# Value loads cut at 112 partitions instead of 115, and one more batch whose expert is chosen from its first token

## The chip, the core and the metric

The kernel runs on one core of a Trainium2 chip. The metric is the device time of one execution, in microseconds (us). The engines are TensorE (PE in the profile, its weight loads PEld), VectorE (DVE), ScalarE (ACT), GpSimd (POOL) and SyncE (SP). DMAs are issued by an engine's queue (SPq, ACTq); sixteen DMA engines move the data.

## What is computed

Eight batches. In each, 8 heads of packed attention (32 packed queries read 576 keys and values, then the 576 queries read the 32 packed results), and then a mixture of experts over the 576 tokens: every token is sent to an expert, which is two matrix products with a relu between.

```python
def sm_attn(qq, kk, vv):
    s = scale * np.matmul(qq, kk.transpose(0, 1, 3, 2))
    s = s - np.max(s, axis=-1, keepdims=True)
    a = np.exp(s)
    a = a / (np.sum(a, axis=-1, keepdims=True) + 1e-09)
    return np.matmul(a, vv)
p_packed = sm_attn(p, k, v)          # 8 batches, 8 heads, 576 tokens, 64 wide; 32 packs
out = sm_attn(q, p_packed, p_packed)
# x = out as [batch, token, 512]; E = 8 experts, w1 [512, 1024], w2 [1024, 512]
logits = np.einsum('bsd,de->bse', x, w_gate)
local_gate = 1.0 / (1.0 + np.exp(-np.einsum('bsd,de->bse', x, w_local).squeeze(-1)))
for s in range(S):
    fresh_e = int(np.argmax(logits[b, s]))
    e = fresh_e if s == 0 or local_gate[b, s] < 0.5 else prev_e
    prev_e = e
    h = np.maximum(x[b, s] @ w1[e], 0.0)
    out[b, s] = p[e] * (h @ w2[e])   # p: softmax of logits[b, s]
```

## The kernel before

The kernel counts on it that all tokens of a batch go to the expert of the batch's first token. It computes that one expert for all 576 tokens, and notes in `stray` whether any token would have gone elsewhere; only then does the branch `general` at the end (line 1053) run.

For each batch the work is a set of Python generators, which a planner (`weave`, line 994) interleaves into one fixed order per engine while the program is built:

- `loads` (line 324) issues the batch's inputs on SP's queue: values (`load_values`, line 277, two loads, for the even and the odd heads, into the tile `kv`), packed queries (`p_in`, line 315), keys and queries (`load_blocks`, line 289, four DMAs each at line 298, into the tile `qn`). Keys and queries come in runs of 32 floats.
- `turn_keys`, `scores` (L414), `keys` (transposes L461, product with the values L474, L489) and `queries` (L535, softmax on DVE and ACT at L565 to L582, then `a2h` and `a2l`, the high and low parts of the attention weights, at L588 and L591) do the attention of a batch.
- `gates` (line 684) computes the logits of all tokens (L692, L700). Out of them `choose` (line 618) takes the expert's number into a register of SP (`value_load`, L627).
- `early_choice` (line 629) takes the expert from the first token alone: it needs the packed results of both halves of the heads (`ppT`) and that token's queries (`q0`, products L642, a short softmax L650 to L665, product with the gate weights L672, argmax L681), and none of the batch's queries. Batches below `FIRST` use it: here 0 and 1. For them `gate_weights` (L607) makes the gate product; for the others L544 makes it inside `queries`.
- `weights` (line 783) waits for that register, then loads the expert's `w1` in two halves (`w1t`, L792) and `w2` in eight pieces (`w2raw`, L801). `pack_weights` multiplies `w1` with the packed results (L818) into `wph` and `wpl`, the weights of the first product.
- `chunks` (line 922) is the main stream: for every batch 8 chunks of 128 columns, each with the first product (`layer1`, L841), relu (L851, L856), the split of `w2` (`split`, L867, L869), and one chunk later the second product (`layer2`, L880, L885, L889). `store` (L920) writes the output.

TensorE executes in program order, so a matmul whose operands are late holds all that stand behind it. Ahead of batch 0's main stream the planner puts in matmuls that nobody reads (`keep_warm`, L211); how many is fixed when the program is built. SP's queue also runs in order: a DMA that waits, or the read of an expert's register at L627, holds the DMAs behind it.

What sets the order around the change, apart from data: a batch's loads start when the previous batch's are all issued and the expert of the one before that is known (line 339); each load needs a free buffer (4 `kv`, 3 `qn`, 2 `p_in`, 8 `w2raw`, 2 `w1t`); and line 348 holds the keys of batch `FIRST` until `w1` of the batch ahead of it has been issued.

576 tokens stand in the values' tile as 5 tokens per partition: 115 partitions hold 575, and partition 115 the last one. So each of the two loads of a batch is one DMA of 115 partitions (575 KB) and one of one partition (1 KB).

Of the kernel before, what the change touches and what calls it, by code (L numbers as in the profile page):

```python
# [19 lines left out]
B, H, S, D = 8, 8, 576, 64  # L20
# [4 lines left out]
TP = 96  # L25
NJ = S // TP
J3 = NJ // 2
NV, VP = 5, 116
HALF = S // 2

NT = HALF // 32
SPAD = 640
NB = SPAD // 128
FIRST = 2
NC = F // 128
TAIL = S - 512

# [118 lines left out]
def packed_attn_moe_kernel(  # L156
# [12 lines left out]
    nc = tc.nc  # L169
# [7 lines left out]
    def tile_(shape, dtype, name, tag=None):  # L177
        bufs = BUFS.get(tag or name, 2)
        x = sb.tile(shape, dtype, name=name, tag=tag or name, bufs=bufs)
        clock.follow(x.tensor.name, tag or name, bufs)  # L180
        return x
# [47 lines left out]
    nc.vector.memset(wgl, 0.0)  # L229
    q0 = [const.tile([64, H, 32], F32, name=f"q0_{x}") for x in range(FIRST)]  # L230
    for x in q0:
# [12 lines left out]
    def at(src, b):  # L244

        return src[b] if isinstance(b, int) else src[bass.ds(b, 1)].squeeze(0)
# [7 lines left out]
    def need(*tiles, slot=(), banks=0, when=None):  # L254
        slots = [(x, 1) if isinstance(x, str) else x for x in ((slot,) if isinstance(slot, str) else slot)]

        def ready():

            if (when is not None and not when()) or not all(clock.free_slot(*x) for x in slots):
                return None  # L260
            free = free_banks()
            if len(free) < banks:
                return None
            return max(clock.ready(tiles), free[banks - 1][0] if banks else 0.0, *(clock.slot(*x) for x in slots))
        ready.banks = banks
        return ready
# [10 lines left out]
    def load_values(src, b, Q):  # L277

        x = tile_([128, HQ, NJ * D], F32, "kv")
        clock.rate = 250.0  # L280
        rows = at(src, b).rearrange("(h q) s d -> q s h d", q=NQ)[Q]
        nc.sync.dma_start(
            out=x[:VP - 1, :, :NV * D].rearrange("p h (c d) -> p h c d", c=NV),
            in_=rows[:S - 1].rearrange("(p c) h d -> p h c d", c=NV),
        )
        nc.sync.dma_start(out=x[VP - 1:VP, :, :D], in_=rows[S - 1:S])
        return x

    def load_blocks(src, b):


        x = tile_([128, H, NT * 32], F32, "qn")
        rows = at(src, b).rearrange("h (c i r) (a j) -> r a i (h c) j", r=2, c=NT, a=2)
        clock.rate = 150.0
        for r in range(2):
            for a in range(2):
                ps_ = slice(64 * r + 32 * a, 64 * r + 32 * a + 32)
                nc.sync.dma_start(out=x[ps_].rearrange("i h (c j) -> i (h c) j", j=32), in_=rows[r, a])  # L298
        return x

    def load_packs(b, queues):

        x = tile_([TP, H, D], F32, "p_in")
        clock.rate = 150.0
        for z, queue in enumerate(queues):
            queue.dma_start(out=x[NP * z:NP * z + NP], in_=at(p, b).rearrange("h n d -> n h d"))
        return x

    def load_packs_by_half(b):

        x = tile_([128, H, D // 2], F32, "p_in")
        clock.rate = 130.0
        halves = at(p, b).rearrange("h n (a j) -> a n h j", a=2)
        for z in range(4):
            nc.sync.dma_start(out=x[NP * z:NP * z + NP], in_=halves[z % 2])
        return x

    def begin(b, st, early=False):
        st["b"], st["early"], st["first"] = b, early, isinstance(b, int) and b < FIRST
        st["gate"] = gate_all[b % 3 if isinstance(b, int) else 0]  # L320
        st["ppT"] = [None] * NQ
        st["quads"] = st["asked"] = st["scored"] = st["weighed"] = st["raised"] = 0

    def loads(st):

        b = st["b"]
        if st["early"]:
            st["p"] = load_packs(b, (nc.sync, nc.scalar, nc.scalar))

            clock.rate = 100.0  # L330
            with nc.allow_non_contiguous_dma(reason="512 elements"):
                for x in range(FIRST):
                    nc.scalar.dma_start(out=q0[x][:, :, 0:1], in_=q[x, :, 0:1, :].rearrange("h s d -> d h s"))
            nc.scalar.dma_start(out=wgl[:, :, 0:E], in_=w_gate.rearrange("(h d) e -> d h e", d=D))
            nc.scalar.dma_start(out=wgl[:, :, E:E + 1], in_=w_local.rearrange("(h d) e -> d h e", d=D))
            order = (("k", 0), ("k", 1), ("v", 0), ("v", 1), ("q", 0), ("q", 1))
        else:
            if isinstance(b, int):
                yield need(when=lambda: "loaded" in sts[b - 1] and (b < 2 or "ereg" in sts[b - 2]))
            order = (("v", 0), ("v", 1), ("p", 1), ("k", 1), ("q", 1))  # L340
        for name, Q in order:
            blocks = name in "qk" and not st["early"]
            if isinstance(b, int) and b == 1 and name == "p":

                yield need(when=lambda: len(sts[0].get("w1", ())) == 2)
            if isinstance(b, int) and b == 1 and name in FIRST_W2:
                yield need(when=lambda: len(sts[0].get("w2", ())) >= FIRST_W2[name])
            if isinstance(b, int) and b == FIRST and name == "k":

                yield need(when=lambda: len(sts[b - 1].get("w1", ())) == 2)  # L350
            yield need(slot="p_in" if name == "p" else "qn" if blocks else "kv")
            if name == "p":
                st["p"] = load_packs_by_half(b)
                continue
            x = {"k": k, "v": v, "q": q}[name]
            if blocks:
                st[name] = load_blocks(x, b)
            else:
                st[name, Q] = (load_tokens if st["early"] else load_values)(x, b, Q)
        st["loaded"] = True  # L360
# [633 lines left out]
    def weave(main):  # L994
# [3 lines left out]
        while main in threads or any(x.batch < 0 for x in threads):  # L998
            while loading < B and loading <= max(at_batch[0], 0) + AHEAD + 1:
                begin(loading, sts[loading], early=(loading == 0))  # L1000
                threads.append(Thread(loads(sts[loading]), loading, True))
                loading += 1
# [50 lines left out]
    with tc.If(found[0] > 0, label="general"):  # L1053
        rows_d = {}
        for name, src in (("codes", codes_all), ("fresh", fresh_all)):
            tp = bank()
            nc.tensor.transpose(
                out=tp[:B * NB, :128], in_=src.rearrange("a b n -> a (b n)"), identity=ident,
# [35 lines left out]
        with tc.For_i(0, B) as bi:  # L1094
            with tc.For_i(0, E) as ei:
                go = nc.values_load(todo[0:1, bass.ds(bi, 1), bass.ds(ei, 1)].rearrange("a b e -> a (b e)"), min_val=0, max_val=1)
                with tc.If(go > 0):
                    st = {}
                    begin(bi, st)
                    drain(slots(st), loads(st), turn_keys(st, 0), turn_keys(st, 1), scores(st, 0), scores(st, 1), keys(st, 0), keys(st, 1), turn_queries(st, 0), turn_queries(st, 1), queries(st, 0), queries(st, 1))  # L1100
                    drain(gates(st, expert=ei), weights(st), pack_weights(st))
                    col = sb.tile([128, NB], F32, name="col", bufs=1)
                    nc.sync.dma_start(out=col, in_=at(ec_d, bi).rearrange("(n t) -> t n", t=128))
                    want = sb.tile([128, 1], F32, name="want", bufs=1)
                    nc.vector.tensor_copy(out=want, in_=code[:, bass.ds(ei, 1)])
                    mask = sb.tile([128, NB], I32, name="mask", bufs=1)
                    nc.vector.tensor_scalar(out=mask, in0=col, scalar1=want, scalar2=None, op0=ALU.is_equal)
                    drain(chunks([(bi, st)], drain, mask))
# [28 lines left out]
```

## Time and profile before

| what | value |
|---|---|
| median of 3 runs | 446.18 us (444.81, 446.18, 743.2) |
| profiled execution | 443.56 us, of which span from first to last instruction 441.8 us |
| PE busy | 422.0 us, 96% of the span |
| DVE, ACT busy | 69%, 41% of the span |
| granted TensorE clock, mean | 0.984 |
| DMA queue of SP and others (q1) | 72.30 MB, 75.7% of sixteen engines |

Times in the rows count from the span's start. A timeline row gives start, duration, engine, line, operation and the count of merged instructions; in brackets stands the idle time of that engine just before, and what ended it. PE is busy nearly everywhere, so its time is to be read by stretches, together with the granted clock (1.00 is 2.4 GHz, 0.50 is 1.2 GHz).

### The profile page before, as it was taken

The numbers are of one execution on the slowest core, as the hardware profiler recorded it, in microseconds if no ns is written. First come the engines' busy times: TensorE is split into PE (matmuls) and PEld (weight loads), VectorE is DVE, ScalarE is ACT, GpSimd is POOL, SyncE is SP. The second block draws the span as 40 slices with busy tenths as digits, with TensorE's granted clock in tenths as the row PEclk, the third lists the DMA queues.
The fourth block names the chain that finished last, engine by engine and source line by source line (L and its number), as shares of the span: only waits on it lengthen the run. The fifth ranks groups of instructions, "written<-read, shape, count | busy, mean of one in ns | idle before, by whom it ended". The sixth has DMA issues, their size and how long they took to land.

```text
span 441.8 us, 9954 instructions
## 1 busy us (share of the span) xinstructions
PE 422.0 (96%) x3834; PEld 325.7 (74%) x3835; DVE 305.9 (69%) x838; ACT 179.4 (41%) x407; POOL 26.2 (6%) x56
## 2 busy tenths in 40 slices
PE   8959999999997999999999999999999999999995
PEld 7746877676785578767876888777876878778883
DVE  4584668968688659868975588868886588544332
ACT  1424243453341653355425354246335444344221
POOL 0001000110011001100110002000110002000000
PEclk9997999999999699999999999999999999999999
DMA  9888965996998779977997797659957030732003
GB/s 188 198 252 187 154 143 165 275 134 126 133 227 191 278 136 131 220 290 134 151 229 289 135 138 196 238 180 128 188 191 260 27 108 1 287 108 94 1 0 111
DMA packets 172448, 73.12 MB, mean 166 GB/s; under 512 B 142662, under 2 KB 151406, under 8 KB 172398
## 3 DMA queue, kind: packets, MB, share of 16 engines
q1 hardware_dynamic: 169742, 72.30, 75.7%
q8 instruction: 31, 0.51, 0.5%
q10 hardware_dynamic: 2656, 0.15, 0.5%
q14 instruction: 19, 0.16, 0.1%
HBM read 63.00 MB, written 9.44 MB: 164 GB/s over the span
## 4 chain that ended last, share of the span: by engine, by line
PE 80%; DMA 7%; DVE 6%; SPq 2%; issue 1%; ACT 1%; ACTq 0%; POOLq 0%; DVEq 0%; POOL 0%
PE acc L880 37%; PE bank L841 21%; PE bank L818 4%; DMA w1t<-in_moe_w_dram 4%; PE acc L885 3%; PE acc L889 3%; PE bank L414 2%; PE bank L474 2%; PE bank L461 2%; PE bank L535 2%; DMA qn<-in_k_dram 2%; SPq L298 2%; PE acc L211 1%; DVE qn L374 1%; DMA p_in<-in_p_dram 1%
## 5 line engine op out<-in xcount | busy, mean ns | idle before, releaser
L880 PE MATMUL acc<-w2s,h 128*128 128x512 f32 x768 | 210.8, 404 | 0.3 <-DVE h L856 0.3
L880 PEld LDWEIGHTS acc<-w2s,h 128*128 128x128 f32 x768 | 135.2, 189 | 35.6 <-issue 12.7
L851 ACT ACTIVATE h<-bank 128x288 fp32r<-128x288 f32 x128 | 52.8, 412 | 114.5 <-PE bank L841 104.2
L856 DVE SCALAR_TENSOR_TENSOR h<-bank,h 128x288 fp32r<-128x288 f32 (+2 forms) x192 | 61.5, 347 | 47.6 <-ACT h L851 47.2
L841 PEld LDWEIGHTS bank<-a2h,wph 128*128 128x128 f32 x256 | 46.3, 189 | 22.9 <-issue 4.0
L841 PE MATMUL bank<-a2h,wph 128*128 128x288 f32 x256 | 57.6, 306 | 1.9 <-DVE df L750 0.8
L841 PE MATMUL bank<-a2l,wph 128*128 128x288 f32 x256 | 55.2, 296 | 0.6 <-POOL a2l L591 0.6
L841 PE MATMUL bank<-a2h,wpl 128*128 128x288 f32 x256 | 55.0, 296 | 0.0
L869 DVE TENSOR_TENSOR w2s<-w2raw,w2s 128x512 fp32r<-128x512 f32 x64 | 47.1, 736 | 4.2 <-ACT w2s L867 4.1
L841 PEld LDWEIGHTS bank<-a2l,wph 128*128 128x128 f32 x256 | 41.2, 189 | 0.8 <-POOL a2l L591 0.8
L591 POOL TENSOR_TENSOR a2l<-a2t,a2h 128x576 fp32r<-128x576 f32 x15 | 21.8, 1454 | 331.4 <-ACT a2h L588 331.4
L841 PEld LDWEIGHTS bank<-a2h,wpl 128*128 128x128 f32 x256 | 41.2, 189 | 0.0
L867 ACT CAST w2s<-w2raw 128x512 fp32r<-128x512 f32 x64 | 39.5, 617 | 0.2
L825 ACT CAST wph<-bank 128x512 fp32r<-128x512 f32 x31 | 16.8, 589 | 37.2 <-PE bank L818 34.2
L828 DVE TENSOR_TENSOR wpl<-bank,wph 128x512 fp32r<-128x512 f32 x31 | 20.0, 684 | 16.1 <-ACT wph L825 16.1
L885 PE MATMUL acc<-w2s,h 128*128 128x512 f32 x64 | 26.8, 418 | 0.0
L889 PE MATMUL acc<-w2s,h 128*64 128x512 f32 x64 | 25.2, 394 | 0.0
L818 PE MATMUL bank<-w1t,ppT 64*32 64x512 f32 x248 | 20.0, 652 | 5.4 <-DMA w1t<-in_moe_w_dram 5.4
L211 PEld LDWEIGHTS acc<-warm 128*128 128x128 f32 x134 | 18.5, 220 | 3.7 <-issue 2.7
L211 PE MATMUL acc<-warm 128*128 128x128 f32 x134 | 20.1, 309 | 1.2 <-DVE warm L204 1.2
L553 DVE STREAM_TRANSPOSE sT<-bank 128x288 f32<-128x288 f32 x29 | 12.4, 463 | 12.1 <-ACT gate L551 9.7
L374 DVE STREAM_TRANSPOSE qn<-qn 128x1152 f32<-128x1152 f32 x14 | 18.9, 1350 | 2.5 <-DMA qn<-in_k_dram 2.5
(152 smaller groups left out, 414.0 us busy)
## 6 DMA issues: line engine op xcount, KB each, us to landing
w1t<-in_moe_w_dram SPq DMA_DIRECT2D x16, 1024.0 KB
w2raw<-in_moe_w_dram SPq DMA_DIRECT2D x64, 256.0 KB
out_dram<-o SPq DMA_DIRECT2D x32, 256.0 KB
qn<-in_k_dram SPq DMA_DIRECT2D x28, 288.0 KB
qn<-in_q_dram SPq DMA_DIRECT2D x28, 288.0 KB
kv<-in_v_dram SPq DMA_DIRECT2D x14, 575.0 KB
kv<-in_k_dram SPq DMA_DIRECT2D x2, 576.0 KB
kv<-in_v_dram SPq DMA_DIRECT2D x2, 576.0 KB
```

The costliest lines, as they stand in the source:

```text
L211: nc.tensor.matmul(out=warm_ps[:, :128], lhsT=warm, rhs=warm, start=True, stop=True)
L374: nc.vector.transpose(out=kT, in_=kT)
L591: eng.tensor_tensor(out=a2l, in0=a2t, in1=a2h.bitcast(F32), op=ALU.subtract)
L818: nc.tensor.matmul(out=ts[Q][32 * h:32 * h + 32, :], lhsT=st["ppT"][Q][rows, 32 * h:32 * h + 32], rhs=w1t[rows, h], start=True, stop=True,)
L841: nc.tensor.matmul(out=t[:, :HALF], lhsT=st["wp"][c // 4][wi][:, Q, fs], rhs=a2[ai][Q][:, ts], start=(n == 0), stop=(n == 5),)
L851: nc.scalar.activation(out=h[:, HALF * half:HALF * half + HALF], in_=t[:, :HALF], func=AF.Relu)
L856: nc.vector.scalar_tensor_tensor(out=h[:, dst:dst + z - a], in0=t[:, a:z], scalar=0.0, in1=h[:, HALF * half + a:HALF * half + z].bitcast(F32),
L867: nc.scalar.copy(out=w[:, 0], in_=raw)
L869: nc.vector.tensor_tensor(out=w[:, 1], in0=raw, in1=w[:, 0].bitcast(F32), op=ALU.subtract)
L880: nc.tensor.matmul(out=acc, lhsT=hs[hi], rhs=w[:, wi], start=(c == 0 and n == 0), stop=(c == NC - 1 and n == 2),)
L885: nc.tensor.matmul(out=acc, lhsT=h[:, 512:S + TAIL], rhs=w[:, 0], start=(c == 0), stop=False, skip_group_check=True,)
L889: nc.tensor.matmul(out=acc[0:TAIL], lhsT=h[:, 512:S], rhs=w[:, 1], start=False, stop=(c == NC - 1), skip_group_check=True,)
```

## The change

Three edits. The values' load of 115 partitions is cut into one of 112 and one of 3 partitions (`VW = 112`); the one of a single partition stays. `FIRST` goes from 2 to 3, so batch 2 too takes its expert from the first token, with a third `q0` tile that is cleared and loaded at the start. And the keys of batches 2 and 3 (before: of batch 2) wait in the planner's order until `w1` of the batch ahead is issued. Batch 0 loads its values by `load_tokens` and is not touched by the first edit.

```diff
-NV, VP = 5, 116
+NV, VP, VW = 5, 116, 112
 HALF = S // 2
...
-FIRST = 2
+FIRST = 3
...
         rows = at(src, b).rearrange("(h q) s d -> q s h d", q=NQ)[Q]
-        nc.sync.dma_start(
-            out=x[:VP - 1, :, :NV * D].rearrange("p h (c d) -> p h c d", c=NV),
-            in_=rows[:S - 1].rearrange("(p c) h d -> p h c d", c=NV),
-        )
+        for lo, hi in ((0, VW), (VW, VP - 1)):
+            nc.sync.dma_start(
+                out=x[lo:hi, :, :NV * D].rearrange("p h (c d) -> p h c d", c=NV),
+                in_=rows[NV * lo:NV * hi].rearrange("(p c) h d -> p h c d", c=NV),
+            )
         nc.sync.dma_start(out=x[VP - 1:VP, :, :D], in_=rows[S - 1:S])
...
-            if isinstance(b, int) and b == FIRST and name == "k":
+            if isinstance(b, int) and 2 <= b <= FIRST and name == "k":
                 yield need(when=lambda: len(sts[b - 1].get("w1", ())) == 2)
```

Every line behind the diff's third hunk is one number higher in the changed kernel. Up to batch 2's packed results TensorE's order is the same in both.

**SP's queue, from batch 3's values on, before** (`e` is batch 2's expert, taken from its gates; the `w1t` under it is batch 2's; `qn<-in_k` and `qn<-in_q` are batch 3's keys and queries):

```order
L282 DMA kv<-in_v_dram 115x4x320
L286 DMA kv<-in_v_dram 1x4x64
L315 DMA p_in<-in_p_dram 32x8x32 x4
L298 DMA qn<-in_k_dram 32x72x32 x4
...
L920 DMA out_dram<-o 64x512
L298 DMA qn<-in_q_dram 32x72x32 x4
L627 TENSOR_LOAD e_1822
L627 ISA x2
L792 ISA
L792 DMA w1t<-in_moe_w_dram 128x4x512
```

The same place in the change (`eix` is batch 2's expert from its first token):

```order
L283 DMA kv<-in_v_dram 112x4x320
L283 DMA kv<-in_v_dram 3x4x320
L287 DMA kv<-in_v_dram 1x4x64
L316 DMA p_in<-in_p_dram 32x8x32 x4
...
L921 DMA out_dram<-o 64x512
L628 TENSOR_LOAD eix
L628 ISA x2
L793 ISA
L793 DMA w1t<-in_moe_w_dram 128x4x512
...
L299 DMA qn<-in_k_dram 32x72x32 x4
L299 DMA qn<-in_q_dram 32x72x32 x4
```

Batch 3's keys and queries now stand behind the read of batch 2's expert, its `w1` and five pieces of its `w2`; before, they stood ahead of all of these.

**TensorE at the end of batch 1's main stream, before**: the scores of batch 3 (L414, two pairs) and batch 2's first product of weights (L818) in one block, with no chunk's matmul between:

```order
L889 MATMUL acc_1418<-w2s,h 64x512
L414 MATMUL bank_1924<-qn,p_in 32x288 x4
L414 MATMUL bank_1925<-qn,p_in 32x288 x4
L414 MATMUL bank_1942<-qn,p_in 32x288 x4
L414 MATMUL bank_1943<-qn,p_in 32x288 x4
L818 MATMUL bank_1966<-w1t,ppT 32x512 x4
L818 MATMUL bank_1967<-w1t,ppT 32x512 x4
L841 MATMUL bank_1988<-a2h,wph 128x288 x2
```

In the change the same scores of batch 3 (L415 there), by which time batch 2's main stream is under way:

```order
L842 MATMUL bank_2036<-a2h,wpl 128x288 x2
L881 MATMUL acc_2055<-w2s,h 128x512 x3
L415 MATMUL bank_2064<-qn,p_in 32x288 x4
L415 MATMUL bank_2065<-qn,p_in 32x288 x4
L881 MATMUL acc_2080<-w2s,h 128x512 x3
L881 MATMUL acc_2084<-w2s,h 128x512 x3
L415 MATMUL bank_2090<-qn,p_in 32x288 x4
L415 MATMUL bank_2091<-qn,p_in 32x288 x4
```

The two pairs of scores are apart, with products of the main stream between them. Batch 2's weights have gone forward into batch 1's main stream:

```order
L881 MATMUL acc_1370<-w2s,h 128x512 x3
L673 MATMUL bank_1674<-gate_103,et 32x32 x2
...
L881 MATMUL acc_1401<-w2s,h 128x512 x3
L819 MATMUL bank_1807<-w1t,ppT 32x512 x4
L819 MATMUL bank_1808<-w1t,ppT 32x512 x4
L886 MATMUL acc_1422<-w2s,h 128x512
```

L673 is the gate product of batch 2's first token and L819 the first use of its `w1`. Between these two stand 18 L842, 21 L881, one L886 and one L890; between L673 and batch 3's first L415 stand 60 L842, 60 L881, 16 L819, 16 of the gates' and 5 each of L886 and L890. For the batch before, both kernels have between L672 and L818 18 L841, 21 L880, 8 L535, one L885 and one L889, and from L672 to batch 2's first L414 54 L841, 60 L880, 16 L818, 8 L535, 16 of the gates' and 4 each of L885 and L889 (in the old line numbers).

## Rows read from the trace of the kernel before

**Rows 1.** The page: the granted clock of TensorE in 40 equal slices of the span, in tenths of full speed.

```profile
PEclk9997999999999699999999999999999999999999
```

**Rows 2.** Busy time by stretches; columns: stretch, its length, busy time of PE, PEld, DVE, ACT, POOL with the count of instructions, granted clock, mean share of the sixteen DMA engines, GB/s.

```profile
28.30:33.60 5.30, 0.01 (x1) 0.00 (x0) 5.15 (x13) 1.19 (x2) 0.00 (x0) 0.80 1.04 347
31.50:38.30 6.80, 4.61 (x28) 2.98 (x29) 3.26 (x8) 2.21 (x4) 0.33 (x1) 0.50 0.82 273
89.00:103.00 14.00, 12.32 (x89) 9.04 (x75) 10.71 (x37) 6.01 (x13) 1.62 (x5) 1.00 1.32 128
138.00:144.10 6.10, 3.74 (x47) 1.08 (x49) 5.78 (x21) 0.00 (x0) 0.00 (x0) 1.00 0.85 302
144.10:151.00 6.90, 6.75 (x28) 3.53 (x28) 5.15 (x14) 4.20 (x9) 0.00 (x0) 0.51 0.96 353
189.00:230.00 41.00, 40.83 (x390) 31.16 (x388) 32.02 (x77) 19.73 (x46) 3.74 (x6) 1.00 1.01 188
```

**Rows 3.** The same columns where loads of one kind fill the queue: batch 0's keys and values (96 partitions, 4:9), then batch 1's values (115 partitions, 21:23), `w1t` (128 partitions, 30:31), and batch 3's values (104:108).

```profile
4.00:9.00 5.00, 4.45 (x39) 4.26 (x38) 2.26 (x2) 1.28 (x1) 0.00 (x0) 1.00 1.14 243
21.00:23.00 2.00, 1.64 (x19) 1.41 (x18) 1.19 (x7) 2.00 (x6) 0.00 (x0) 1.00 0.33 120
30.00:31.00 1.00, 0.00 (x0) 0.00 (x0) 0.96 (x5) 0.00 (x0) 0.00 (x0) 1.00 1.03 373
104.00:108.00 4.00, 4.00 (x37) 3.04 (x36) 3.83 (x10) 1.33 (x4) 0.00 (x0) 1.00 0.33 121
```

**Rows 4.** SP's queue in order of time, while it issues batch 1's second value load and batch 0's `w1t`.

```profile
18.65 0.28 SPq L282 DMA_DIRECT2D kv<-in_v_dram  x1
18.98 3.11 SPq L286 DMA_DIRECT2D kv<-in_v_dram  x1
24.45 1.04 SPq L792 DMA_DIRECT2D w1t<-in_moe_w_dram  x2
```

**Rows 5.** TensorE in order of time, from batch 0's queries to its main stream.

```profile
24.92 3.39 PE L211 MATMUL acc<-warm 128*128 128x128 f32 x28
...
33.69 1.96 PE L818 MATMUL bank<-w1t,ppT 64*32 64x512 f32 x16 [5.38 <-DMA w1t<-in_moe_w_dram]
...
35.58 4.25 PE L211 MATMUL acc<-warm 128*128 128x128 f32 x24
...
41.14 0.43 PE L841 MATMUL bank<-a2l,wph 128*128 128x288 f32 x2
```

**Rows 6.** VectorE, ScalarE and GpSimd in order of time, on the way to the operands of that first L841.

```profile
33.00 0.84 DVE L582 STREAM_TRANSPOSE a2t<-sT 128x288 f32<-128x288 f32 x2
...
35.68 1.07 ACT L825 CAST wph<-bank 128x512 fp32r<-128x512 f32 x2 [6.18 <-PE bank L818]
...
36.63 1.26 ACT L588 CAST a2h<-a2t 128x576 fp32r<-128x576 f32 x2
...
37.35 0.76 DVE L591 TENSOR_TENSOR a2l<-a2t,a2h 128x576 fp32r<-128x576 f32 x1 [3.51 <-ACT a2h L588]
...
37.97 1.42 POOL L591 TENSOR_TENSOR a2l<-a2t,a2h 128x576 fp32r<-128x576 f32 x1 [36.25 <-ACT a2h L588]
...
38.02 1.28 DVE L828 TENSOR_TENSOR wpl<-bank,wph 128x512 fp32r<-128x512 f32 x2
```

**Rows 7.** From batch 1's early choice to batch 2's scores, TensorE, SP's queue and VectorE in order of time.

```profile
70.29 0.31 PE L672 MATMUL bank<-gate,et 128*32 128x32 f32 x4
...
72.61 1.07 SPq L792 DMA_DIRECT2D w1t<-in_moe_w_dram  x2
...
77.73 12.49 SPq L298 DMA_DIRECT2D qn<-in_k_dram  x4
...
79.30 1.09 PE L818 MATMUL bank<-w1t,ppT 64*32 64x512 f32 x16
...
96.28 1.38 DVE L374 STREAM_TRANSPOSE qn<-qn 128x1152 f32<-128x1152 f32 x1 [2.46 <-DMA qn<-in_k_dram]
...
99.91 0.69 PE L414 MATMUL bank<-qn,p_in 64*32 64x288 f32 x8
```

**Rows 8.** Batch 2's weights and batch 3's scores: SP's queue and TensorE in order of time.

```profile
137.63 1.01 SPq L792 DMA_DIRECT2D w1t<-in_moe_w_dram  x2
...
139.10 0.92 PE L414 MATMUL bank<-qn,p_in 64*32 64x288 f32 x16 [0.57 <-issue]
...
140.81 0.69 PE L414 MATMUL bank<-qn,p_in 64*32 64x288 f32 x8 [0.79 <-DVE gsm L759]
...
142.50 0.69 PE L414 MATMUL bank<-qn,p_in 64*32 64x288 f32 x8 [1.00 <-DVE a L424]
...
143.00 2.43 PE L818 MATMUL bank<-w1t,ppT 64*32 64x512 f32 x16
```

**Rows 9.** What touches the tile `kv` from SP's queue: count, then shortest, median and longest time in which one holds the queue (ns), first and last start.

```profile
L282 SPq DMA_DIRECT2D kv<-in_v_dram x14: 275/354/1415, 15.4 to 288.3; - x14
L286 SPq DMA_DIRECT2D kv<-in_v_dram x14: 632/3554/5059, 15.7 to 288.7; - x14
```

**Rows 10.** Groups by line: the operations of an early choice and the one that it replaces.

```profile
L544 PE MATMUL bank<-wgl,ppT 64*32 64x9 f32 x96 | 2.7, 172 | 0.0
...
L607 PE MATMUL bank<-wgl,ppT 64*32 64x32 f32 x32 | 0.6, 193 | 0.0
...
L642 PE MATMUL bank<-q,ppT 64*32 64x32 f32 x16 | 0.3, 198 | 0.0
```

## The prediction

> **What bounds the kernel now.** I looked at the stretches first, then at the clock, then at who waits for whom at the places where TensorE (PE) loses time. In the middle of the run it loses almost nothing: between 189 and 230 us it is busy 40.83 of 41.00 us at full clock [rows 2]. The rest of the kernel runs on DVE, ACT and DMA under this cover, so a faster transfer pays only where PE stands still or runs at half clock. There are three such places.
>
> First, 28.3 to 33.6: PE is busy 0.01 of 5.30 us [rows 2]. It waits 5.38 us for batch 0's first half of `w1` (`w1t`), and finds the clock at 0.50, that is 1.2 GHz, from 31.5 to 38.3 [rows 2, 5]. Second, 89 to 103: 1.68 us idle, around a DVE that stood 2.46 us for batch 2's keys [rows 2, 7]. Third, 138 to 144.1: 2.36 us idle in three gaps ahead of and between batch 3's scores, and behind them 6.9 us at a clock of 0.51 [rows 2, 8]. The dip of the clock shows in the slices too, twice in the run [rows 1].
>
> **Why `w1t` is late at the start.** SP issues it at 24.45, PE gets it just before 33.69: 9.2 us [rows 4, 5]. Batch 2's `w1t` is issued at 137.63 and used at 143.00, by a matmul that shows no wait for it: at most 5.4 us [rows 8]. What stands ahead of the first one are batch 1's values, the second load issued at 18.65 [rows 4]. While values alone run, the sixteen DMA engines are busy 0.33 of the time and move 120 GB/s; loads of 96 and 128 partitions keep all of them busy and move 243 and 373 GB/s [rows 3]. A share of 0.33 is 5.3 engines of sixteen. So two loads of 575 KB (1.18 MB) need 9.8 us, last until about 28.5, and hold `w1t`'s share of those engines back, while eleven others idle.
>
> The Trainium skill, page "DMA: Bandwidth & Descriptors", section "Why a DMA increments its semaphore by 16 and not by 1", says that a DMA is spread over the largest number of engines, up to 16, that divides its outermost count. By it 115 partitions get 5, 112 get 16 and 3 get 3; the trace agrees for 115 (5.3), and no row of before has 112.
>
> **Edit 1, at the start.** The cost of a 112-partition load is bounded by 120 GB/s (as 115) and 373 (as 128); the nearest row is that of 96 partitions, with 243. At that rate the two loads take 4.8 us and are done by 23.5, ahead of `w1t`'s issue. Then `w1t` lands like batch 2's, 5.4 us after issue: 29.9 in place of 33.6. What is late next:
> - PE: L818 1.09 us at full clock (as at 79.30), the 24 fillers L211 at 3.39/28 us each, 2.9, then the 1.4 us that lie between the second L818's place and the L841 at 41.14: 35.3 [rows 5, 7]. (From the end of the fillers, 35.58 + 4.25 = 39.8, to 41.14 are 1.3 to 1.4.)
> - The operands: `a2t` is finished at 33.84 by a DVE chain that doesn't need `w1t`. Behind it come half of ACT's 1.26 us for `a2h` and POOL's 1.42 for `a2l`: 35.9. DVE needs 0.76 and 1.28 for its `a2l` and `wpl`: also 35.9 [rows 6].
>
> The later path is that of the operands: 41.14 less 35.9 is 5.2 us. If the clock still falls at 31.5, the fillers take 4.25 and the L818 behind them twice as long: about 37.4, a gain of 3.7. If PE's path decides: 5.8. I take 5.2, since most of the long wait ahead of the fall is gone. For batch 1's keys and queries to keep up, their queue must move forward as well; it does, since their DMAs stand behind the same `w1t`.
>
> **Edit 1, elsewhere.** The values of batches 3 to 7 come while PE is covered: nothing. On SP's queue the one-partition piece holds the queue 3.55 us in the median and 0.63 at the least [rows 9]; I read the long ones as waiting behind the 115-partition piece on the same few engines. With that gone, three short pieces take no more of SP than two did.
>
> **Edits 2 and 3, around batch 2's weights and batch 3's scores.** Batch 2's `w1t` was issued at 137.63, out of its gates. Now it follows its early choice. Batch 1 shows the pattern: L672 at 70.29, `w1t` issued at 72.61 (2.3 later), first L818 at 79.30 without waiting (9.0 later), keys of the next batch issued behind it and landed at 96.28 (23.7 after `w1t`), scores at 99.91 [rows 7].
>
> Does L819 of batch 2 wait? By the order in the section on the change it has the same cover as batch 1's L818 less 8 L535. Products of that shape take 0.92 us per 16 records [rows 8], so the cover is 8.1 us against 2.3 + 5.4 = 7.7. It just holds; each us that the choice comes later than that is one of PE's.
>
> The block of scores and weights at 138 to 144 is taken apart: scores stand between products of the main stream. Removed: 2.36 us idle and half of 6.9 us at half clock, 3.4; less the 0.2 that a quiet stretch has: 5.5 [rows 2]. Added: batch 3's keys now stand on SP's queue behind the read of batch 2's expert, `w1t` and five `w2raw`, so they land 23.7 less one `w2raw` (256 KB at 373 GB/s, 0.7 us) after `w1t`'s issue: 25.3 after L673. The scores came 3.6 us behind the keys' landing, so 28.9. Work of PE up to there is 29.6 less the 1.68 that it idled, 27.9, and little more in the change. So 0 to 1.2 us of PE are lost; I take 0.8. Net: 4.7, between 0 (the stop and the slow clock only move) and 5.5.
>
> The second place, batch 2's keys, stays: their `w1t` hangs on batch 1's choice as before, and moves with PE.
>
> **Small terms.** Batch 2 gets 16 records of L642 (0.3 us), 16 of L607 (0.3) and 4 of L672 (0.3) on PE and loses 16 of the 96 L544 (0.45): 0.4 us more [rows 7, 10]. The dozen small DVE operations lie between L642 and L673, beside the main stream; without that cover they would cost the 2.3 us above. The third `q0` clears and loads before PE has data. The planner lays out batches 3 to 7 anew; PE's idle there is 0.2 of 41 us [rows 2], so I take 0, with -0.5 to +1.5.
>
> **Sum.** Profiled execution 443.56 - 5.2 - 4.7 + 0.4 = 434.1 us. The two ordinary runs, 444.81 and 446.18, are 1.25 and 2.62 above the profiled one; with the mean of 1.9 the time is 436.0, 2.3% under the median of 446.18.
>
> **Rivals.**
> - *The values were not what held `w1t`, or 112 partitions run no wider than 115.* For it: no row has 112. Against: the share of 0.33 in each stretch of values and never elsewhere. Edit 1 gives nothing: 434.1 + 5.2 + 1.9 = 441.2. Chance 0.10.
> - *Batch 3's stop moves instead of going*: keys two us later than I worked out, and the clock falls behind the gap again. For it: batch 2's keys are late already, 2.46 us [rows 7]. 434.1 + 4.7 + 1.9 = 440.7. Chance 0.15.
> - *Small pieces cost by the piece.* If each 3-partition piece holds SP 3.55 us like the one-partition piece [rows 9], `w1t` is issued at about 27.0 instead of 24.45 and edit 1 gives some 1.5 us: 434.1 + 3.7 + 1.9 = 439.7. Against: the shortest such hold is 0.63 us. The Trainium skill, same page, section "Rules for kernel authors", speaks for this one: below 64 KB a transfer is mostly overhead, and pieces are to be joined. The 1 KB pieces here do hold SP longer than the 575 KB ones (3.55 against 0.35 us), but the spread up to 5.06 looks like a queue ahead of them rather than a fixed price. Chance 0.06.
> - *The other side: slower than before.* SP executes in order, and in the change the read of batch 2's expert stands ahead of batch 3's keys and queries. If DVE comes to the early choice late by x, `w1t` and the keys are late by x, and PE stops at L819 or at the scores; behind such a stop the clock can fall too, as at 144, for 3.4 us more. It outweighs the 9.5 us of gains from x of about 6 us on; with x = 10 it gives 434.1 + 10 + 3.4 + 1.9 = 449.4. For it: DVE is busy 5.78 of 6.10 us at such a place [rows 2]. Against: in batch 1 the whole way took 2.3. Chance 0.04.
> - *Neither place gains*: 445.9. Chance 0.05.
>
> **How the numbers follow.** My forecast has 0.60, with a range of its own of 432 to 439 (start 3.7 to 5.8, batch 3 down to 3, later batches -0.5 to +1.5). Faster by over 2%, about what a measurement of this kernel can tell from no change, is below 437.3: three quarters of my forecast, 0.45. The first three rivals and the one without gain lie within 2%, and slower by over 2% (455.1) needs an x of over 15: 0.02. The range takes in the first three rivals and leaves out the last two and the edges: 432.0 to 441.5.
>
> **What would show it.** Values alone at a DMA share near 1 instead of 0.33; L818 of batch 0 near 30 and no half clock there; the L841 of 41.14 near 36; `w1t` of batch 2 issued near 117, L819 and batch 3's scores with gaps under 1 us, and no slow clock near 140. A share of 0.33 that stays, or a DVE that waits several us for batch 3's keys, would make it wrong.

## The result and the profile after

| | median, us | runs | ratio to before, 95% interval |
|---|---|---|---|
| before | 445.83 | 444.81, 446.18, 445.48 (and 743.2) | |
| changed | 433.75 | 435.34, 433.21, 434.06, 433.43 | 0.9742 [0.9705, 0.9780] |

The changed kernel is 2.6% faster. Its profiled execution took 435.34 us with a span of 433.6, and is the slowest of the four. The same kernel was run again beside the experiments (e12 below) and came out at 0.9748 [0.9721, 0.9775], with a profiled execution of 434.08 us. Some executions of a kernel are slow ones (743.2 here, five of e10's ten): the ratios leave them out, the medians count them.

Lines of the changed kernel stand one higher than before from the value loads on (L282 is now L283, L818 is L819, L841 is L842). Where rows of before answer, their group is named.

Busy time by stretches of the changed kernel, with the columns of [rows 2]. The first two stretches are those of batch 1's values, the third the gap ahead of the first `w1` product, the fourth the place of the first slow clock, then batch 2's keys, batch 3's scores, and the quiet stretch.

```profile
19.00:21.00 2.00, 1.95 (x39) 1.53 (x38) 0.79 (x4) 1.25 (x4) 0.00 (x0) 1.00 1.10 240
21.00:23.00 2.00, 1.34 (x16) 1.22 (x14) 1.19 (x6) 1.79 (x5) 0.00 (x0) 1.00 1.07 263
...
28.80:31.00 2.20, 0.37 (x10) 0.21 (x17) 2.12 (x5) 1.35 (x2) 0.00 (x0) 1.00 1.00 376
32.00:36.00 4.00, 4.00 (x22) 4.00 (x23) 3.97 (x10) 2.39 (x4) 0.67 (x1) 0.57 1.01 335
88.00:101.00 13.00, 11.97 (x72) 8.99 (x72) 10.25 (x37) 6.11 (x13) 0.51 (x5) 1.00 1.31 130
140.00:152.00 12.00, 12.00 (x89) 9.16 (x90) 10.94 (x42) 6.71 (x16) 0.77 (x3) 1.00 1.15 158
189.00:230.00 41.00, 41.00 (x393) 31.76 (x391) 34.70 (x93) 18.44 (x43) 3.29 (x6) 1.00 1.01 222
```

At 21 to 23 us the values now fill the sixteen DMA engines (1.07, 263 GB/s) where they kept a third of them busy (0.33, 120 GB/s) [rows 3]. Batch 3's place, three gaps and then 6.9 us at half clock before [rows 2, 8], is one stretch in which TensorE (PE) is busy 12.00 of 12.00 us at full clock. Batch 2's keys still cost about a microsecond (11.97 of 13.00).

TensorE of the changed kernel in order of time, in brackets the idle time before a row and what ended it; answers to [rows 5], [rows 7] and [rows 8].

```profile
21.78 0.71 PE L510 MATMUL acc<-ident,kv 96*128 96x96 f32 x6 [0.66 <-DMA kv<-in_q_dram]
...
23.17 0.31 PE L673 MATMUL acc<-gate,et 128*32 128x32 f32 x4
...
30.85 1.09 PE L819 MATMUL bank<-w1t,ppT 64*32 64x512 f32 x16 [1.83 <-DMA w1t<-in_moe_w_dram]
31.88 4.57 PE L211 MATMUL acc<-warm 128*128 128x128 f32 x24
...
37.77 0.43 PE L842 MATMUL bank<-a2l,wph 128*128 128x288 f32 x2
...
117.85 0.31 PE L673 MATMUL bank<-gate,et 128*32 128x32 f32 x4
...
126.00 1.09 PE L819 MATMUL bank<-w1t,ppT 64*32 64x512 f32 x16
...
146.05 0.80 PE L415 MATMUL bank<-qn,p_in 64*32 64x288 f32 x16
```

The wait for batch 0's `w1t` fell from 5.38 to 1.83 us. Batch 2's L819 and batch 3's L415 show no wait. A new wait of 0.66 us has come at 21.78, for batch 0's second queries. In this execution the clock still fell, from about 32.4 to 35.8 us, and the 24 fillers L211 took 4.57 us.

A second new wait stands in batch 0's main stream: VectorE (DVE) waits for batch 1's keys, and TensorE then for VectorE. Before, the same transpose of the keys (at 50.46) shows no wait, and TensorE none there.

```profile
48.63 1.38 DVE L375 STREAM_TRANSPOSE qn<-qn 128x1152 f32<-128x1152 f32 x1 [1.46 <-DMA qn<-in_k_dram]
...
52.15 0.51 PE L842 MATMUL bank<-a2h,wph 128*128 128x288 f32 x2 [0.84 <-DVE h L857]
```

SP's queue of the changed kernel, batch 1's values and batch 0's `w1t`, then batch 2's `w1t` and batch 3's keys (start, time in which SP is held, count).

```profile
15.33 0.77 SPq L283 DMA_DIRECT2D kv<-in_v_dram  x2
16.16 0.73 SPq L287 DMA_DIRECT2D kv<-in_v_dram  x1
18.91 0.73 SPq L283 DMA_DIRECT2D kv<-in_v_dram  x2
19.69 0.60 SPq L287 DMA_DIRECT2D kv<-in_v_dram  x1
25.16 1.70 SPq L793 DMA_DIRECT2D w1t<-in_moe_w_dram  x2
...
119.83 1.05 SPq L793 DMA_DIRECT2D w1t<-in_moe_w_dram  x2
...
123.80 12.28 SPq L299 DMA_DIRECT2D qn<-in_k_dram  x4
```

Batch 0's `w1t` is issued later than before (25.16 against 24.45 [rows 4]) and lands earlier: 5.7 us later instead of 9.2. Batch 2's is issued at 119.83 instead of 137.63 [rows 8], 2.0 us after its L673.

The tile `kv` on SP's queue in the changed kernel: count, shortest, median and longest hold in ns [rows 9].

```profile
L283 SPq DMA_DIRECT2D kv<-in_v_dram x28: 247/368/2348, 15.3 to 278.7; - x28
L287 SPq DMA_DIRECT2D kv<-in_v_dram x14: 586/616/730, 16.2 to 279.4; - x14
```

The one-partition piece (L287), 3.55 us in the median before, now takes 0.62, and 0.73 at most. L283 mixes the pieces of 112 and of 3 partitions.

### The profile page after: what moved, and what is told of

Its sections match the earlier page's. It is cut to its first block, busy times and chain, and to the rows that moved or that the text cites. A ratio compares the mean times of both kernels' runs of the same rounds, so it can differ in the third digit from the quotient of the medians.

```text
span 433.6 us, 10026 instructions
## 1 busy us (share of the span) xinstructions
PE 418.6 (97%) x3854; PEld 324.1 (75%) x3855; DVE 306.9 (71%) x850; ACT 178.6 (41%) x407; POOL 26.9 (6%) x56
## 4 chain that ended last, share of the span: by engine, by line
PE 77%; DMA 10%; DVE 5%; SPq 5%; issue 2%; POOLq 0%; ACTq 0%; POOL 0%; DVEq 0%; ACT 0%
PE acc L881 37%; PE bank L842 21%; SPq L299 3%; PE acc L886 3%; PE acc L890 3%; PE bank L819 3%; DMA w2raw<-in_moe_w_dram 3%; PE bank L475 2%; DMA kv<-in_q_dram 2%; PE bank L536 2%; PE bank L415 2%; PE bank L462 2%; DMA qn<-in_k_dram 2%; DVE qn L375 2%; DMA w1t<-in_moe_w_dram 2%
## 5 line engine op out<-in xcount | busy, mean ns | idle before, releaser
L881 PE MATMUL acc<-w2s,h 128*128 128x512 f32 x768 | 208.8, 402 | 0.1
L881 PEld LDWEIGHTS acc<-w2s,h 128*128 128x128 f32 x768 | 134.6, 188 | 31.8 <-issue 9.0
L842 PEld LDWEIGHTS bank<-a2h,wph 128*128 128x128 f32 x256 | 45.6, 188 | 25.9 <-issue 8.8
L842 PE MATMUL bank<-a2h,wph 128*128 128x288 f32 x256 | 57.6, 306 | 3.1 <-DVE df L751 1.3
L842 PE MATMUL bank<-a2l,wph 128*128 128x288 f32 x256 | 55.1, 296 | 0.6 <-POOL a2l L592 0.6
L842 PE MATMUL bank<-a2h,wpl 128*128 128x288 f32 x256 | 54.7, 295 | 0.0
L842 PEld LDWEIGHTS bank<-a2l,wph 128*128 128x128 f32 x256 | 40.9, 188 | 1.0 <-POOL a2l L592 0.8
L842 PEld LDWEIGHTS bank<-a2h,wpl 128*128 128x128 f32 x256 | 41.0, 188 | 0.0
L886 PE MATMUL acc<-w2s,h 128*128 128x512 f32 x64 | 26.7, 417 | 0.0
L890 PE MATMUL acc<-w2s,h 128*64 128x512 f32 x64 | 25.2, 394 | 0.0
L375 DVE STREAM_TRANSPOSE qn<-qn 128x1152 f32<-128x1152 f32 x14 | 19.1, 1361 | 4.4 <-DMA qn<-in_k_dram 4.4
L211 PE MATMUL acc<-warm 128*128 128x128 f32 x134 | 20.8, 317 | 1.2 <-DVE warm L204 1.2
L211 PEld LDWEIGHTS acc<-warm 128*128 128x128 f32 x134 | 19.2, 228 | 2.9 <-issue 1.9
L464 ACT COPY a1T<-bank 116x384 f32<-116x384 f32 (+2 forms) x29 | 12.0, 430 | 19.2 <-PE bank L462 18.9
L521 DVE STREAM_TRANSPOSE qn<-qn 128x1152 f32<-128x1152 f32 x14 | 19.1, 1367 | 0.2 <-DMA kv<-in_v_dram 0.2
```

The costliest lines, as they stand in the source:

```text
L211: nc.tensor.matmul(out=warm_ps[:, :128], lhsT=warm, rhs=warm, start=True, stop=True)
L375: nc.vector.transpose(out=kT, in_=kT)
L842: nc.tensor.matmul(out=t[:, :HALF], lhsT=st["wp"][c // 4][wi][:, Q, fs], rhs=a2[ai][Q][:, ts], start=(n == 0), stop=(n == 5),)
L881: nc.tensor.matmul(out=acc, lhsT=hs[hi], rhs=w[:, wi], start=(c == 0 and n == 0), stop=(c == NC - 1 and n == 2),)
L886: nc.tensor.matmul(out=acc, lhsT=h[:, 512:S + TAIL], rhs=w[:, 0], start=(c == 0), stop=False, skip_group_check=True,)
L890: nc.tensor.matmul(out=acc[0:TAIL], lhsT=h[:, 512:S], rhs=w[:, 1], start=False, stop=(c == NC - 1), skip_group_check=True,)
```

## Experiments

Diffs are against the changed kernel. Gains in us are (1 - ratio) times the median of before measured beside the run, with the interval worked out in the same way.

### e1 to e4: the parts by themselves

```diff
 e1_split_only       -FIRST = 3
                     +FIRST = 2
 e2_choice_only      -        for lo, hi in ((0, VW), (VW, VP - 1)):
                     +        for lo, hi in ((0, VP - 1),):
 e3_split_b1         as e1, with the cut for batch 1 alone
 e4_split_rest       as e1, with the cut for batches 2 to 7 alone
```

> The cut at 112 alone, FIRST = 2; TensorE and VectorE have exactly the order of the kernel before. Theory (two separate gains: batch 0's w1 comes sooner, and batch 3's scores no longer stop TensorE): only the first gain, 2 to 4 us, so 441.5 to 443.5; w1t waits TensorE 1 to 2.5 us instead of 5.4; the stop at 138 to 144 and the half clock behind it stay. Rival (the values were also what held up batch 2 and 3): 434 to 437.

> FIRST = 3 and the later keys alone, values still in pieces of 115 and 1; TensorE and VectorE have exactly the order of the change. Theory: only the second gain, 6 to 9 us, so 437 to 440; TensorE still waits 5 us for batch 0's w1t with the half clock behind it. Rival (the early choice needs the faster values): 441 to 445, with waits at batch 2's L818 or batch 3's scores.

> The cut at 112 for batch 1's values alone, FIRST = 2. Theory: all that the cut gives is at the start, so the same as the cut in all batches to 1 us: 441.5 to 443.5. Rival (it is the sum over seven batches): a seventh of the gain, 445.

> The cut at 112 for batches 2 to 7 alone, FIRST = 2. Theory: nothing, 444.5 to 446.5, since those loads lie under work of TensorE. Rival (sum over the batches): 442 to 443.

| run | median, us (before: 444.22) | ratio | gain, us |
|---|---|---|---|
| e1, edit 1 alone | 438.45 | 0.9880 [0.9850, 0.9910] | 5.3 [4.0, 6.7] |
| e2, edits 2 and 3 alone | 439.42 | 0.9910 [0.9875, 0.9946] | 4.0 [2.4, 5.6] |
| e3, edit 1 in batch 1 | 439.79 | 0.9911 [0.9877, 0.9946] | 4.0 [2.4, 5.5] |
| e4, edit 1 in batches 2 to 7 | 444.24 | 1.0013 [0.9988, 1.0039] | -0.6 [-1.7, 0.5] |

On TensorE, VectorE, ScalarE and GpSimd the instructions of e1, e3 and e4 stand in the order of before, and those of e2 in that of the change, so the differences are those of the DMAs and of the order, each by itself. Edit 1 earns its time in batch 1's values; in the other batches it earns nothing that can be seen.

Busy time of the two places in e1 (edit 1 alone), with the columns of [rows 2]: first the place of the first slow clock, then batch 3's.

```profile
32.70:39.50 6.80, 6.36 (x83) 4.92 (x82) 6.47 (x13) 3.88 (x9) 1.80 (x5) 1.00 1.22 256
138.50:145.40 6.90, 6.52 (x34) 3.31 (x35) 6.05 (x23) 3.51 (x8) 0.00 (x0) 0.51 1.05 391
```

And the same two in e2 (edits 2 and 3 alone).

```profile
32.70:39.50 6.80, 5.75 (x34) 4.11 (x35) 3.18 (x6) 2.21 (x4) 1.46 (x4) 0.50 0.81 234
138.50:145.40 6.90, 6.90 (x66) 5.67 (x65) 5.26 (x13) 3.01 (x6) 2.36 (x5) 1.00 1.19 130
```

Each part clears its own place and leaves the other's half clock as it was. The product of the two ratios is 0.979, about 9.3 us; the whole measured 11.2 [10.0, 12.4] in e12. The half-widths, 1.4, 1.6 and 1.2 us, make 2.4 together (root of the sum of squares), so the 1.9 us between are not shown to be anything.

### e5, e6, e7: how the values are cut

```diff
-NV, VP, VW = 5, 116, 112
+NV, VP, VW = 5, 116, 110        # e5_cut110: pieces of 110, 5 and 1
+NV, VP, VW = 5, 116, 113        # e6_cut113: pieces of 113, 2 and 1
-        for lo, hi in ((0, VW), (VW, VP - 1)):
+        for lo, hi in (*((x, x + 16) for x in range(0, VW, 16)), (VW, VP - 1)):   # e7_sixteens
```

> The change with pieces of 110, 5 and 1 partitions. Theory (a load runs on the largest number of engines up to 16 that divides its partitions: 110 on 10): values alone at a DMA share of 0.6 to 0.7 and some 230 GB/s, still done before batch 0's w1t is issued, so 433 to 435.5. Rival (it is the size of the piece that counts, and 110 runs as wide as 112): a share near 1 and the same time. Rival (110 is no better than 115): a share of 0.33 and 437 to 440.

> The change with pieces of 113, 2 and 1 partitions; 113 has no divisor up to 16. Theory: each load of 565 KB runs on one engine at about 24 GB/s, 24 us each and 48 us a batch, and every other transfer waits for that engine's share: 550 to 700 us, TensorE idle for tens of us per batch, DMA share under 0.1 while values run alone. Rival (only more than some number of partitions, or full groups of 16, matters): 433 to 440.

> The change with each piece of 112 partitions cut into seven of 16: nine DMAs a load, 18 a batch in place of 6. Theory (a short piece holds SP 0.35 us and is otherwise free): 4 us more of SP per batch, under other work; w1t of batch 0 at most 0.5 us later, 433 to 435.5. Rival (small pieces cost by the piece, 2 to 3.5 us each in the queue): w1t of batch 0 10 us or more later and 450 us or more.

| run | median, us (before: 444.71) | ratio |
|---|---|---|
| e5, 110 + 5 + 1 | 433.59 | 0.9748 [0.9716, 0.9779] |
| e6, 113 + 2 + 1 | 685.17 | 1.5416 [1.5353, 1.5479] |
| e7, seven of 16, 3 + 1 | 447.30 | 1.0046 [1.0015, 1.0076] |

Busy time of e6 where values load; the DMA share and the rate are the last two columns.

```profile
24.00:26.00 2.00, 2.00 (x40) 1.24 (x39) 0.99 (x3) 0.02 (x1) 0.00 (x0) 1.00 0.07 24
...
40.00:60.00 20.00, 0.00 (x0) 0.00 (x0) 0.00 (x0) 0.00 (x0) 0.00 (x0) 0.50 0.07 24
```

One partition more than 112 brings the share to 0.07, 1.1 engines of sixteen, and 24 GB/s. The two loads of batch 1 then hold SP's queue for 21.11 and 22.95 us, so that `w1t` is issued at 62.56 only:

```profile
15.58 21.11 SPq L283 DMA_DIRECT2D kv<-in_v_dram  x2
...
37.59 22.95 SPq L283 DMA_DIRECT2D kv<-in_v_dram  x2
```

Here a piece of 2 partitions stands behind one of 113, as the one-partition piece stood behind 115 before. All waiting of TensorE for `w1t` is this (engine, line, waited for: total us, times, longest):

```profile
PE bank L819 <- DMA w1t<-in_moe_w_dram: 134.6, 7, 43.8
```

The same columns as before for e5, values at 110 partitions:

```profile
21.00:23.00 2.00, 1.86 (x22) 1.49 (x19) 1.31 (x7) 1.74 (x7) 0.00 (x0) 1.00 0.76 195
23.00:25.00 2.00, 2.00 (x44) 1.51 (x42) 0.56 (x5) 1.02 (x3) 0.00 (x0) 1.00 0.76 196
```

So 113, 115, 110 and 112 partitions give 24, 120, 195 and 263 GB/s: the rate doesn't go with the size, and the share of 110 is between those of 115 and 112. By the rule of the Trainium skill, page "DMA: Bandwidth & Descriptors", section "Why a DMA increments its semaphore by 16 and not by 1", these counts get 1, 5, 11 and 16 engines (the largest divisor up to 16), which makes shares of 0.06, 0.31, 0.69 and 1.00, an estimate. The traces agree with 0.07, 0.33, 0.76 and 1.07, all a little above it. (The expectation of e5 put 110 on 10 engines; 11 divides it too.) At 195 GB/s the values are out of the way as well, and e5's time is that of the change.

e7 sends the same bytes, sixteen partitions at a time. SP's queue of e7, then TensorE's wait.

```profile
15.96 6.41 SPq L283 DMA_DIRECT2D kv<-in_v_dram  x8
22.41 0.74 SPq L287 DMA_DIRECT2D kv<-in_v_dram  x1
23.26 4.81 SPq L283 DMA_DIRECT2D kv<-in_v_dram  x8
28.12 0.61 SPq L287 DMA_DIRECT2D kv<-in_v_dram  x1
30.10 1.05 SPq L793 DMA_DIRECT2D w1t<-in_moe_w_dram  x2
```

```profile
35.17 1.96 PE L819 MATMUL bank<-w1t,ppT 64*32 64x512 f32 x16 [5.83 <-DMA w1t<-in_moe_w_dram]
```

Eight pieces, seven of 16 partitions and one of 3, take 4.81 us of SP's queue, 0.60 each. `w1t` goes out at 30.10 instead of 25.16, and TensorE waits 5.83 us for it. All told e7 is some 13 us slower than the change (by the ratios), more than edit 1 gains: its profile has 10.4 us of waiting for `w1t` in three places (the change: 1.8 in one) and half clock for 6.8 us twice, from 34.5 and from 239.3. I had taken a third of a microsecond a piece and no harm; that fell. The rival price, some 2 to 3.5 us a piece, was too high.

### e8, e10: the early choice and the order of SP's queue

```diff
-            if isinstance(b, int) and 2 <= b <= FIRST and name == "k":
+            if isinstance(b, int) and b == 2 and name == "k":          # e8_keys3_not_held
-FIRST = 3
+FIRST = 8                                   # e10_first8, keys held for b 2 and 3 as in the change
```

> The change without its third edit for batch 3: batch 3's keys and queries stand on SP's queue ahead of the read of batch 2's expert. Theory (what helps is that batch 2's w1 comes early, which needs SP's queue free at that moment; keys and queries ahead of it take 18 us of the queue): w1t of batch 2 issued 5 to 10 us later than in the change, TensorE waits at L819 or does it later, 434.5 to 439. Rival (the order on SP does not matter there, since the queue idles from 110 to 120): 432.5 to 434.5, and no wait of VectorE for batch 3's keys.

> The change with FIRST = 8: every batch takes its expert from its first token; the keys of batches 2 and 3 are held as in the change, no others. Theory (from batch 3 on TensorE is busy all the time, so a sooner choice has nothing to give): 433 to 436. Rival (each boundary gains like batch 2's): 415 to 425.

e8 took 437.85 us, 0.9828 [0.9790, 0.9866] of before's 444.95; the change, measured beside it, 434.19. By the ratios that is 3.6 us, with half-widths of 2.1 together. SP's queue of e8, then TensorE.

```profile
119.83 6.87 SPq L299 DMA_DIRECT2D qn<-in_q_dram  x4
127.73 1.81 SPq L793 DMA_DIRECT2D w1t<-in_moe_w_dram  x2
```

```profile
118.64 0.31 PE L673 MATMUL bank<-gate,et 128*32 128x32 f32 x4
...
134.75 1.09 PE L819 MATMUL bank<-w1t,ppT 64*32 64x512 f32 x16 [2.58 <-DMA w1t<-in_moe_w_dram]
```

Without edit 3, batch 3's queries stand ahead of batch 2's `w1t`: it is issued 9.1 us after its L673 instead of 2.0, and TensorE stops for 2.58 us. The early choice needs the queue free in front of it. Its size isn't clean: e8's profile has a longer wait at the start as well (3.7 us for batch 0's `w1t`, with the clock falling), which the edit has no visible reason to cause, and the planner laid out the later work anew.

e10, the early choice for all batches, took 449.39 us, 1.0024 [0.9982, 1.0066] of before, by the ratios some 12 us more than the change; I had expected about no difference to the change. TensorE of e10, two new waits at the start:

```profile
15.86 1.49 PE L462 MATMUL acc<-ident,a 128*96 128x128 f32 x6 [2.53 <-ACT a L450]
...
24.36 0.33 PE L608 MATMUL bank<-wgl,ppT 64*32 64x32 f32 x16 [1.09 <-DMA wgl<-in_moe_w_local_dram]
```

Eight loads of `q0` hold ACT's queue for 8.82 us ahead of its first work, where the prediction had let a third one in for nothing. The waits for `w1t` add up to 6.7 us in three places. The L842 that stands at 36.97 in e12 stands at 41.17 in e10, so 4.2 us of the 14.0 between their profiles arise at the start; the other 9.8 were not taken apart.

### e9, e11: two tries to gain more

```diff
-            order = (("v", 0), ("v", 1), ("p", 1), ("k", 1), ("q", 1))
+            order = (("p", 1), ("k", 1), ("v", 0), ("v", 1), ("q", 1)) if isinstance(b, int) and b == 1 \
+                else (("v", 0), ("v", 1), ("p", 1), ("k", 1), ("q", 1))        # e9_values_behind_keys
+            if isinstance(st["b"], int) and st["b"] in (1, 2):                 # e11_keys_ahead_of_w2
+                yield need(when=lambda: c < 2 or "k" in sts[st["b"] + 1])
             yield need(slot="w2raw")
```

> The change with batch 1's loads in another order: packs and keys, then values, then queries; the other batches as in the change. Theory (on sixteen engines batch 1's values delay the landing of batch 0's second queries by 0.7 us, and batch 0's choice with it): batch 0's L673 0.5 to 0.8 us sooner, w1t issued near 24.4; if batch 1's values still land in time, 432.5 to 433.5. Rival (the values are then late for batch 1's product with them, or push the queries): a wait of some us at batch 1's L475 or L536, 435 to 440.

> The change, and in batches 1 and 2 only two of the eight pieces of w2 are loaded ahead of the next batch's keys, the others behind them. Theory (the next losses are VectorE's waits of 2.2 and 0.7 us for the keys of batches 2 and 3, which stand behind 3.7 MB of w1 and w2): keys land 2 to 3 us sooner, those waits go, 431.5 to 433.5. Rival (w2's later pieces then come too late, or TensorE's idle is elsewhere): 434 to 436.

e9: 441.49 us, 0.9919 [0.9880, 0.9957], slower than the change. Its planner laid out batch 1 anew: its queries came late, and the clock fell near 68 and from 92 to 99 us. The 0.66-us wait that it was made for is gone all the same: batch 0's second queries go through without a gap, and the first token's gate product (L674 there) stands 2.6 us behind its L644, as before, instead of 3.1 in the change. TensorE of e9:

```profile
20.86 0.91 PE L511 MATMUL acc<-ident,kv 96*128 96x96 f32 x9
...
22.87 0.31 PE L674 MATMUL acc<-gate,et 128*32 128x32 f32 x4 [0.35 <-DVE et L667]
```

e11: 434.62 us, 0.9753 [0.9716, 0.9790], the same as the change. Batch 2's keys land 5 us earlier (3 of them counted from the issue of batch 1's `w1t`), but the planner moved the work that reads them as well, and VectorE waits as before (e11's trace, in order of time):

```profile
88.92 1.38 DVE L375 STREAM_TRANSPOSE qn<-qn 128x1152 f32<-128x1152 f32 x1 [2.01 <-DMA qn<-in_k_dram]
```

### e12: the change again

> The change itself, unedited, beside the same runs of the kernel before. Theory (the two gains add up: 1.2% and 0.9% from the parts alone): a ratio of 0.976 to 0.981. Rival (they help each other): 0.970 to 0.975.

434.19 us (433.92 to 434.39), 0.9748 [0.9721, 0.9775]. TensorE of this execution:

```profile
22.46 0.71 PE L510 MATMUL acc<-ident,kv 96*128 96x96 f32 x6 [0.74 <-DMA kv<-in_q_dram]
...
31.20 1.09 PE L819 MATMUL bank<-w1t,ppT 64*32 64x512 f32 x16 [1.50 <-DMA w1t<-in_moe_w_dram]
32.23 2.94 PE L211 MATMUL acc<-warm 128*128 128x128 f32 x24
...
36.62 0.51 PE L842 MATMUL bank<-a2h,wph 128*128 128x288 f32 x2 [0.43 <-DVE wpl L829]
36.97 0.29 PE L842 MATMUL bank<-a2l,wph 128*128 128x288 f32 x1
```

The fillers take 2.94 us, so the clock did not fall here, after a wait of 1.50 us instead of 1.83. In e3 it did not fall after a longer one either:

```profile
30.74 1.09 PE L819 MATMUL bank<-w1t,ppT 64*32 64x512 f32 x16 [1.92 <-DMA w1t<-in_moe_w_dram]
31.76 2.94 PE L211 MATMUL acc<-warm 128*128 128x128 f32 x24
```

## Why the prediction was right

It forecast 436.0 us (432.0 to 441.5); measured were 433.75 and 434.19. By its own steps:

- **Values keep two thirds of the engines idle and hold `w1t` back.** Shown. The share went from 0.33 to 1.07, `w1t` lands 5.7 and 5.4 us after its issue (25.16 to 30.85 here, 25.84 to 31.20 in e12; taken: 5.4), and e3 and e4 place the gain in batch 1's values. The rival that 112 run no wider falls with the 263 GB/s. One profile departs: in e8, with the values as wide, `w1t` took 7.8 us (24.82 to 32.64), and the cause of that stays open.
- **The start, 5.2 us (3.7 to 5.8).** e1: 5.3 [4.0, 6.7]. In the profiles the L842 that answers to the L841 at 41.14 [rows 5] stands at 37.77 with the slow clock (37.4 was worked out for that case) and at 36.97 without it (35.9). So 3.4 and 4.2 us were gained up to there. The operands decide in e12, as foreseen (0.43 us of waiting for `wpl`). What fell short is the step that their chain stays where it was: the first token's L673 stands 1.4 us later in e12 (23.85 against 22.46), `a2t` is finished 1.4 us later (35.24 against 33.84), and `w1t`, 2.0 us behind L673 in both, goes out at 25.84 instead of 24.45. Of these 1.4 us, 0.5 come from the new wait for batch 0's second queries, which the prediction lacks. The other 0.9 stand already at L643 ahead of it (20.69 against 19.82), and no run tells why.
- **The wait for batch 0's second queries is edit 1's own.** The kernels that load batch 1's values at 112 partitions in one piece ahead of the keys, with this start (the change, e12, e1, e3, e8, e11), show it, 0.36 to 0.75 us, and e7 with its pieces of 16 shows 0.76. Before, e2 and e4, which leave batch 1 at 115, do not; in e5 with 110 the row of those transposes is 0.3 us longer (1.22 instead of 0.91), none of which reaches L673. With the values moved behind the keys it is gone (e9). So loads that fill all engines held back one that was issued before them. How the engines share is not shown.
- **Batch 1's keys.** The prediction had them keep up, since their queue moves forward with `w1t`. They do not quite: VectorE waits 1.46 us for them and TensorE 0.84 behind it, a term that the sum put at nothing. e1, e3 and e12 have the same 0.84.
- **Edits 2 and 3, 4.7 less 0.4.** e2: 4.0 [2.4, 5.6]. The steps came out closely: `w1t` 2.0 us behind L673 (2.3), L819 8.15 behind it (a cover of 8.1) and without a wait, batch 3's scores 28.2 behind it (28.9). The keys land late for VectorE as foreseen, but 23.5 us behind L673 instead of the 25.3 worked out, and TensorE loses none of the 0.8 us taken for that:

```profile
141.33 1.38 DVE L375 STREAM_TRANSPOSE qn<-qn 128x1152 f32<-128x1152 f32 x1 [0.71 <-DMA qn<-in_k_dram]
```

That row is VectorE of the changed kernel. The rival that batch 3's stop moves instead of going needed keys 2 us later than worked out; no run tried that. The stop of 2.58 us in e8 is another one, at batch 2's weights: it shows what edit 3 is for.

- **Small pieces.** The 3.55 us of the one-partition piece were a queue behind 115 partitions, as read: 0.62 now. The price by the piece is real but small, 0.6 us of SP (e7). The Trainium skill, page "DMA: Bandwidth & Descriptors", section "Rules for kernel authors", which speaks against transfers below 64 KB, does not decide here: cutting 15 KB off a 575-KB load is worth 4 us in batch 1 (e3), and pieces of 80 KB, above its bound, lose it again (e7).
- **Where 2 us of the time went.** The sum for a profiled execution was 434.1; the two were 435.34, with a slow clock that the other three runs' mean clocks (0.997 to 0.998 against 0.994) speak against, and 434.08. That the latter meets the sum is in part luck: the start was 1.1 us short at L842 and batch 1's keys cost 0.8, and about as much came in behind them: the 0.8 not lost at batch 3's scores, and 1.1 that no run takes apart. The step of the sum that was mis-sized is the last one: 1.9 us were added for the distance of ordinary runs to the profiled one. Measured later, before's medians are 444.22 to 444.95, 0.7 to 1.4 above its 443.56, and the change's runs show no such distance. Without those 1.9 us the sum alone, 434.1, lies beyond 2% (chance given: 0.45).
- **Slips in the working.** 2.36 + 3.4 - 0.2 is 5.6, not 5.5. And the 2.3 us named for the dozen small VectorE operations between L642 and L673 are those from L672 to the issue of `w1t`, behind them; no term rests on it.

## What to carry to other kernels

Look at the share of DMA engines while one kind of load runs alone: a share of a third, or of 0.07, meant here that its partition count divides badly, and the price showed at the transfer behind it, not at the load itself. Cut such a load into one large piece with a count that fills the engines and a small rest, not into many equal ones, since in e7 each piece took 0.6 us of its queue. When a register decides a load early, keep from that queue whatever could stand between the decision and its DMA (here 2.0 us against 9.1).

## What was not expected of the hardware

- A DMA of 113 partitions moves 24 GB/s, a tenth of one of 112; a kernel with fourteen such loads takes 1.54 times as long.
- The length of the wait ahead of it does not settle whether the clock falls. After 1.83 us it fell to half for 3.4 us, after 1.92 in e3 it didn't, nor after 1.74 in e1, 1.57 in e5 and 1.50 in e12; after 3.70 in e8 and 5.38 before it did, for 6.8 us. No run here tells what decides it.
- Pieces in a row cost SP more than one alone: eight take 4.81 us of its queue, 0.60 each, though a single one holds it for 0.42 in the median (e7), and the load of 115 partitions did for 0.35 before [rows 9].
